# Placing the rows of z in SBUF: blocks of 64, 8, 8, 8 and 2 rows, or five of 16 and one of 10

## The chip, the cores and the metric

The kernel runs on one core of a Trainium2 chip. The metric is the time on the device in microseconds (us). Times come from several runs of the whole kernel and, for the profile, from one execution recorded by the hardware profiler. The core has a matrix engine (PE), three engines for elementwise work (DVE, ACT, POOL), a queue engine (SP) that issues most transfers, and 16 DMA engines that carry them out. SBUF is the on-chip memory of 128 partitions; PSUM takes the results of matmuls.

## The reference

The reference chains two blocks. The first is a long causal convolution by FFT, for each of 8 sequences of 5696 positions and 128 channels; the second is a soft mixture of experts over all 45568 positions with 32 slots and 8 experts. All values are float32.

```python
L = 2 * S
Xf = np.fft.rfft(x, n=L, axis=1); Hf = np.fft.rfft(h, n=L, axis=0)
y = np.fft.irfft(Xf * Hf[None], n=L, axis=1)[:, :S, :]
x = y.reshape(B * S, D)
logits = x @ phi
d = softmax over the positions; slot_input = d.T @ x
slot_out[e] = np.maximum(slot_input[e] @ w1[e], 0) @ w2[e]
c = softmax over the slots;  return c @ slot_out
```

(The two softmax lines are put in words here; each subtracts the maximum and adds 1e-9 to the sum.)

## The kernel before

The transform is done as a two-stage transform with N1 = 90 and N2 = 64, written as matmuls with tables of cosines and sines. Stage A (`load_x`, `fold`, `first_stage`) loads x in chunks of 4 columns, folds them on POOL, multiplies by the table s1 on PE (L217), and stores the result to DRAM as f (L226): 60 rows of 4 KB in each of two stores for the low part, 30 rows in each of four for the high part. Stage B (`load_g`, `stage_b1`, `stage_b2`) loads f back as g (L253), multiplies on PE (L267), multiplies by the spectrum of h on DVE (L285, L294), multiplies on PE again (L309) and stores the result to DRAM as z (L318) in packets of 1 KB. Stage C does the last transform and the experts' softmaxes. It goes by pairs T = 0 to 31, two chunks of one sequence each: four pairs make a sequence.

A pair's z is 90 rows of 16 KB. `load_pair` (L338) loads them into a tile of 128 partitions, "zc", by one DMA for every block that `z_blocks` (L18) lists: first row r, number of rows n, first partition p and step between partitions. The rows of the table i1, with which stage_c1 multiplies, are put on the same partitions by `transform_tables` (L54), from the same list, and the table is zero on the partitions without a row. The tile zc is set to zero once, at the start, so the empty partitions contribute zeros. `stage_c1` (L352) then does 16 matmuls per pair (L365), each over the partitions of zc, and combines their results on ACT, DVE and POOL. `stage_c2` transposes on PE (L393), `stage_c3` makes logits, `stage_c4` to `stage_c6` transpose and keep the softmax's parts, and `dispatch` accumulates the slots' inputs (L480).

The work is interleaved by hand. One step t issues the stages in the order of two strings, `ORDER_E = "xXYf1wb5s"` for odd t and `ORDER_O = "zPxXfb26db3m"` for even t: "z" is `load_pair` of the next pair, "P" the loads of g, "x" and "X", "Y" are stage A, "b" is stage B, "1" is stage_c1. Two steps make one pair. All of these DMAs but a few at the start are issued by SP, in program order, and an issue that waits holds up those after it. As long as stages A and B run, `zring` holds one tile, so z of a pair is loaded into the tile from which the pair before was read.

When stages A and B are over, their tiles are given back, and a second tile for z, "zd", is made (L650). Its empty partitions have to hold zeros as well. The kernel uses only the first 96 partitions of it (`used`, L644): `stage_c1` reads `kr = used` partitions when its tile is zn (L354), and of those 96 the six without a row (`held`, L645) are copied from zc by one DMA (L651). After that, `zring` has two tiles; the remaining pairs are loaded alternately into both (L654, L674, L689, L707). The last phase computes the experts and writes the output.

The block list of the kernel before, with n = 90:

```python
left = [(64 + 8 * j, min(8, n - 64 - 8 * j), j, 4) for j in range((n - 57) // 8)]
return [(0, 64, 32, 1)] + left
```

That is rows 0 to 63 on partitions 32 to 95; rows 64 to 71 on partitions 0, 4, ..., 28; rows 72 to 79 on 1, 5, ..., 29; rows 80 to 87 on 2, 6, ..., 30; rows 88 and 89 on 3 and 7.

Of the kernel before, what the change touches and what calls it, by code (L numbers as in the profile page):

```python
# [16 lines left out]

def z_blocks(n):  # L18

    left = [(64 + 8 * j, min(8, n - 64 - 8 * j), j, 4) for j in range((n - 57) // 8)]  # L20
    return [(0, 64, 32, 1)] + left


def transform_tables(S, N1, N2, CH, X0):
# [29 lines left out]
    for r, n, p, step in z_blocks(N1):  # L54
        i1[p:p + (n - 1) * step + 1:step, :, 0:NP] = part[r:r + n]
# [22 lines left out]
def kernel(  # L78
# [24 lines left out]
    nc = tc.nc  # L103
    P = 128
    B, S, D = x.shape
    NSL = moe_phi.shape[1]
    E, _, F = moe_w1.shape
    SPE = NSL // E
    NFC = F // P
    N1, N2 = 90, 64  # L110
# [8 lines left out]
    HP = P // 2  # L119
# [21 lines left out]
    i1 = const.tile([P, 3, HP], F32, name="i1")  # L141
# [31 lines left out]
    def bank():  # L173
        rings.append(rings.pop(0))
        return rings[-1].tile([P, 512], F32, name="bank", tag="bank")
# [146 lines left out]


    zs, ys, Ls, ds = {}, {}, {}, {}
    zn = used = None
    ybufs = [ypool.tile([P, Q * CH, D + 1], F32, name=f"y{i}") for i in range(2)]
    zring = [ypool.tile([P, 2, 2, CH, 2, D], F32, name="zc")]
    lt = ypool.tile([P, CH, 2, HP], F32, name="lt")
# [9 lines left out]
    def load_pair(T):  # L338
        if T >= NT:
            return  # L340
        b, j = divmod(T, NQ)
        t_ = zring.pop(0)
        zring.append(t_)
        w_ = 2 * 2 * CH * 2 * D
        for r, n, p, step in z_blocks(N1):
            nc.sync.dma_start(
                out=t_[p:p + (n - 1) * step + 1:step, :, :, :, :, :].rearrange("k h o n c d -> k (h o n c d)"),
                in_=zd[b].rearrange("q (a r) c d -> (q a) (r c d)",
                                    a=2)[r:r + n, j * w_:(j + 1) * w_])
        zs[T] = t_  # L350

    def stage_c1(T, between):  # L352
        t_ = zs.pop(T)
        kr = used if t_ is zn else P  # L354
        y_ = ybufs.pop(0)
        ybufs.append(y_)

        def part(v, f):
            k = (2 * v + f) * CH
            return y_[:, k:k + CH, 0:D] if f == 0 else y_[:, k + CH - 1:k - 1:-1, 0:D]  # L360

        def product(o, tab, q):
            p = bank()
            for h_ in range(2):
                nc.tensor.matmul(p[h_ * HP:(h_ + 1) * HP, :], i1[0:kr, tab, :],  # L365
                                 t_[0:kr, h_, o, :, q, :], start=True, stop=True)
            return p[:, :].rearrange("p (n d) -> p n d", d=D)

        def fold_out(even, minus, plus):
            nc.vector.tensor_tensor(out=plus, in0=even, in1=minus, op=AL.add)  # L370
            nc.vector.tensor_tensor(out=minus, in0=even, in1=minus, op=AL.subtract)

        b_, a_ = product(0, 1, 1), product(0, 0, 0)
        nc.scalar.activation(part(0, 0), b_, AF.Copy)
        fold_out(a_, part(0, 0), part(1, 0))
        between()
        b_, a_ = product(1, 1, 0), product(1, 2, 1)
        nc.scalar.activation(om[:, :, :], b_, AF.Copy)

        def after():  # L380
            fold_out(a_, om[:, :, :], op[:, :, :])
            for v, o_, eng in ((1, op, nc.gpsimd), (0, om, nc.vector if tail else nc.gpsimd)):
                for part_, sign in ((part(v, 1), AL.subtract), (part(v, 0), AL.add)):
                    eng.tensor_tensor(out=part_, in0=part(v, 0), in1=o_[:, :, :], op=sign)  # L384

        ys[T] = y_
        return after
# [182 lines left out]
    for t in range(last_front + 1):  # L570
# [12 lines left out]
        def slot_b():  # L583
# [19 lines left out]
            "d": lambda: dispatch(pair(3)) if pair(3) is not None else None,  # L603
            "b": lambda: slot_b(),
            "1": lambda: after.append(stage_c1(T, lambda: stage_c4(U) if U is not None else None))
            if T is not None else stage_c4(U) if U is not None else None,
            "w": lambda: [a_() for a_ in after],
# [30 lines left out]
        if NA < t <= NA + E:  # L638
# [2 lines left out]


    T = V + 1
    used = sum(z_blocks(N1)[0][1:3])  # L644
    held = slice(N1 // 64 * 8 + 3, used - 64, 4)  # L645
    front.close()
    rings.append(mid.enter_context(tc.tile_pool(name="ps2", bufs=4, space=PSUM)))
    last = work.enter_context(tc.tile_pool(name="last", bufs=1))
    tail["last"] = last
    zn = last.tile([P, 2, 2, CH, 2, D], F32, name="zd")  # L650
    nc.sync.dma_start(out=zn[held, :, :, :, :, :].rearrange("k h o n c d -> k (h o n c d)"),  # L651
                      in_=zring[0][held, :, :, :, :, :].rearrange("k h o n c d -> k (h o n c d)"))
    zring.insert(0, zn)
    load_pair(V + 2)  # L654
    nc.sync.dma_start(out=w1s[:, E - 1, :], in_=moe_w1[E - 1])
# [7 lines left out]
    y_ = tail["pool"].tile([P, Q * CH, D + 1], F32, name="y2", tag="y2", bufs=1)  # L663

    after = stage_c1(T, lambda: stage_c4(V))
    after()
    stage_c5(V)
    list(softmax(V))
    nc.gpsimd.memset(y_[:, :, D:D + 1], 1.0)
    for q in range(Q):  # L670
        r = slice(q * NSL, (q + 1) * NSL)
        nc.gpsimd.tensor_copy(out=rep4[r, :, :],
                              in_=ident[r, r].unsqueeze(1).broadcast_to([NSL, Q, NSL]))
    load_pair(T + 2)  # L674
    assert (B - 1) * NQ == T + 1
    for V in range(T, NT):
# [10 lines left out]
        if N < NT:  # L687
            after = stage_c1(N, lambda: stage_c4(V))
            load_pair(N + 2)  # L689
        else:  # L690
            stage_c4(V)
# [16 lines left out]
        else:  # L708
            for b in range(2 * (V - T - 1), min(2 * (V - T), B - 2)):
                nc.sync.dma_start(out=tail["cT"][:, b, :, :].rearrange("p r j -> p (r j)"),  # L710
                                  in_=cd[b].rearrange("p r j -> p (r j)"))
            for i in range(4 * (V - T - 1), min(4 * (V - T), E), 2):
                nc.sync.dma_start(
                    out=w2s[:, i:i + 2, :, :],
                    in_=moe_w2[i:i + 2].rearrange("e (p c) d -> p e c d", p=P))
# [5 lines left out]
    p = bank()  # L721
# [8 lines left out]
    p = bank()  # L730
# [11 lines left out]
    for g in range(EG):  # L742
        for f0 in range(0, F, FH):
            p = bank()
# [9 lines left out]
    for g in range(EG):  # L754
        for k0 in range(0, NFC, 4):
            p = bank()
            for k in range(4):
# [3 lines left out]
                out=hidT[:, g, k0:k0 + 4, :], in_=p[:, :].rearrange("p (k c) -> p k c", k=4))  # L761
    sop = bank()
    for g in range(EG):
        for k in range(NFC):
            for q in range(Q):
                nc.tensor.matmul(sop[q * NSL:(q + 1) * NSL, 0:D],
                                 hidT[:, g, k, q * NSL:(q + 1) * NSL], w2s[:, g * Q + q, k, :],
                                 start=(g == 0 and k == 0), stop=(g == EG - 1 and k == NFC - 1))
# [3 lines left out]
    p = bank()  # L772
    nc.tensor.matmul(p[:, 0:D], tail["rep4"][:, :, :].rearrange("p q s -> p (q s)"), so[:, :],
                     start=True, stop=True)
# [16 lines left out]
    for b in range(B):  # L791
        w1 = 0
        for n in (1, 2, 4, 4) if b == 0 else (4, 4, 3):
# [11 lines left out]
            for q in range(Q):  # L805
# [8 lines left out]
                out=ov[b, t0:t0 + n * RW * N2, :].rearrange("(w p n) d -> p w (n d)", p=P, n=CH),  # L814
                in_=o_[:, 0:n, :, :].rearrange("p w q d -> p w (q d)"))
            if lone:
                nc.sync.dma_start(
                    out=ov[:, NV * RW * N2:, :].rearrange("b (j n) d -> b j (n d)", n=CH),
                    in_=o_[:, n, :, :].rearrange("p q d -> p (q d)"))
# [29 lines left out]
```

## Time and profile before

| | us |
|---|---|
| median of 3 runs | 864.13 |
| lowest and highest run | 862.6, 869.32 |
| profiled execution, its own time | 866.8 |
| its span, first to last instruction | 864.8 |
| PE busy | 777.0 (90%) |
| DVE busy | 618.1 (71%) |
| ACT busy | 437.7 (51%) |
| POOL busy | 392.6 (45%) |

The transfers that matter here, from the page's list of DMA issues (destination and source, number, size of each): z into zc, 30 of 1024 KB, 90 of 128 KB and 30 of 32 KB; z into zd, 2 of 1024 KB, 6 of 128 KB and 2 of 32 KB; zeros from zc to zd, one of 96 KB. In all, 272 MB are moved in 153244 packets.

Busy time of an engine is the union of its instructions' times. The slices are 40 equal parts of the span, 21.6 us each, with the busy share in tenths. A line such as L365 is a line of the kernel. The chain of waits follows the work that ended last back through what released each step. The idle time of an engine that doesn't set the pace costs nothing.

### The profile page before, as it was taken

The numbers are of one execution on the slowest core, as the hardware profiler recorded it, in microseconds if no ns is written. First come the engines' busy times: TensorE is split into PE (matmuls) and PEld (weight loads), VectorE is DVE, ScalarE is ACT, GpSimd is POOL, SyncE is SP. The second block draws the span as 40 slices with busy tenths as digits, with TensorE's granted clock in tenths as the row PEclk, the third lists the DMA queues.
The fourth block names the chain that finished last, engine by engine and source line by source line (L and its number), as shares of the span: only waits on it lengthen the run. The fifth ranks groups of instructions, "written<-read, shape, count | busy, mean of one in ns | idle before, by whom it ended". The sixth has DMA issues, their size and how long they took to land.

```text
span 864.8 us, 20506 instructions
## 1 busy us (share of the span) xinstructions
PE 777.0 (90%) x7796; PEld 376.9 (44%) x7796; DVE 618.1 (71%) x929; ACT 437.7 (51%) x967; POOL 392.6 (45%) x372
## 2 busy tenths in 40 slices
PE   5888888788999999999999999999987888978882
PEld 1122333234444444444444444444444454445882
DVE  3058877666877878887888788777879886963542
ACT  2432344344656565665566566655644445562531
POOL 4453424245556556665566555556434332541000
PEclk9999999999999999999999999999999889997755
DMA  9888999999999999999999999999987887760998
GB/s 297 265 284 300 317 328 339 336 335 342 329 316 343 341 345 324 346 334 338 322 336 348 329 342 334 344 326 345 349 298 269 285 306 261 273 267 7 370 381 328
DMA packets 153244, 272.00 MB, mean 315 GB/s; under 512 B 11878, under 2 KB 110054, under 8 KB 150005
## 3 DMA queue, kind: packets, MB, share of 16 engines
q1 hardware_dynamic: 152571, 270.38, 90.2%
q8 instruction: 62, 1.02, 0.5%
q10 hardware_dynamic: 576, 0.31, 0.1%
q14 instruction: 35, 0.29, 0.1%
HBM read 142.57 MB, written 127.98 MB: 313 GB/s over the span
## 4 chain that ended last, share of the span: by engine, by line
PE 65%; DVE 13%; DMA 8%; issue 4%; POOL 2%; ACT 1%; SPq 1%; DVEq 0%; ACTq 0%; POOLq 0%
PE bank L217 17%; PE bank L365 13%; PE bank L309 8%; PE bt L267 8%; PE bank L393 6%; DMA out_dram<-o 5%; PE bank L480 3%; DVE p L285 3%; DVE bt L285 3%; DVE yf L294 3%; PE bank L402 2%; DMA zc<-z 2%; PE bank L431 2%; POOL x L206 1%; PE bank L454 1%
## 5 line engine op out<-in xcount | busy, mean ns | idle before, releaser
L206 POOL TENSOR_TENSOR x<-xc 128x512 f32<-128x512 f32 x144 | 180.1, 1274 | 229.6 <-PE bank L217 209.2
L217 PE MATMUL bank<-x,s 128*32 128x512 f32 (+1 forms) x1152 | 229.5, 611 | 17.5 <-POOL x L206 15.8
L315 ACT ACTIVATE zst<-bank 128x512 f32<-128x512 f32 (+1 forms) x184 | 98.6, 585 | 182.2 <-PE bank L309 166.7
L220 ACT ACTIVATE fst<-bank 128x512 f32<-128x512 f32 x216 | 127.5, 598 | 110.7 <-PE bank L217 95.9
L285 DVE TENSOR_TENSOR p<-bt,Hi 128x1024 f32<-128x1024 f32 x96 | 111.3, 1159 | 34.1 <-PE bt L267 33.3
L365 PE MATMUL bank<-zc,i 128*64 128x512 f32 x480 | 118.1, 614 | 8.5 <-DMA f<-fst 5.0
L217 PEld LDWEIGHTS bank<-x,s 128*32 128x32 f32 (+1 forms) x1152 | 55.9, 124 | 158.8 <-issue 74.9
L309 PE MATMUL bank<-yf,vt 64*64 64x256 f32 x1440 | 101.6, 389 | 26.0 <-DVE yf L294 25.8
L294 DVE TENSOR_TENSOR yf<-bt,p 128x512 f32<-128x512 f32 x192 | 119.3, 663 | 3.3
L267 PE MATMUL bt<-gt,wt 64*64 64x256 f32 x1620 | 113.5, 388 | 3.7 <-DMA gt<-f 2.8
L285 DVE TENSOR_TENSOR bt<-bt,Hr 128x1024 f32<-128x1024 f32 x96 | 113.0, 1177 | 0.0
L267 PEld LDWEIGHTS bt<-gt,wt 64*64 64x64 f32 x1620 | 54.0, 132 | 78.2 <-issue 35.3
L384 POOL TENSOR_TENSOR y<-y,op 128x512 f32<-128x512 f32 x64 | 77.9, 1217 | 9.8 <-DVE op L370 6.7
L309 PEld LDWEIGHTS bank<-yf,vt 64*64 64x64 f32 x1440 | 56.6, 135 | 57.0 <-issue 28.9
L370 DVE TENSOR_TENSOR y<-bank,y 128x512 f32<-128x512 f32 x32 | 22.1, 692 | 72.5 <-PE bank L365 69.5
L393 PE MATMUL bank<-ident,y 109*128 109x109 f32 x512 | 63.9, 276 | 1.3 <-DVE y L384 1.0
L384 POOL TENSOR_TENSOR y<-y,om 128x512 f32<-128x512 f32 x54 | 64.0, 1184 | 2.1
L365 PEld LDWEIGHTS bank<-zc,i 128*64 128x64 f32 x480 | 30.4, 137 | 71.9 <-issue 47.5
L393 PEld LDWEIGHTS bank<-ident,y 109*128 109x128 f32 x512 | 53.5, 149 | 17.8 <-issue 11.5
L395 ACT ACTIVATE yt<-bank 128x360 f32<-128x360 f32 x128 | 51.3, 492 | 3.2 <-PE bank L393 3.0
L802 PE MATMUL op<-so,cT 32*128 32x128 f32 x704 | 46.2, 380 | 5.5 <-ACT o L811 5.0
L285 DVE TENSOR_TENSOR p<-bt,turn 128x1024 f32<-128x1024 f32 (+1 forms) x12 | 14.2, 1179 | 47.5 <-PE bt L267 46.7
(95 smaller groups left out, 802.0 us busy)
## 6 DMA issues: line engine op xcount, KB each, us to landing
gt<-f SPq DMA_DIRECT2D x99, 512.0 KB
z<-zst SPq DMA_DIRECT2D x88, 512.0 KB
f<-fst SPq DMA_DIRECT2D x144, 240.0 KB
zc<-z SPq DMA_DIRECT2D x30, 1024.0 KB
xc<-in_x_dram SPq DMA_DIRECT2D x64, 320.0 KB
f<-fst SPq DMA_DIRECT2D x144, 120.0 KB
out_dram<-o SPq DMA_DIRECT2D x16, 1024.0 KB
zc<-z SPq DMA_DIRECT2D x90, 128.0 KB
```

What stands on the lines that cost most here:

```text
L206: nc.gpsimd.tensor_tensor(out=y_[:, :, :], in0=t_[:, 0, :, :], in1=t_[:, 1, ::-1, :], op=AL.subtract if comp else AL.add)
L217: nc.tensor.matmul(p[o * width:(o + 1) * width, :], s1[:, comp + G, k], folded[(c, comp)][:, :, :].rearrange("p n d -> p (n d)"), start=Tr ...
L220: nc.scalar.activation(st[:, :, G, :], p[:, :].rearrange("p (n d) -> p n d", d=D), AF.Copy)
L267: nc.tensor.matmul(bt[q * HP:(q + 1) * HP, a, o, :], wt[r, 2 * i + q, :], t_[r, 2 * o + q, :, :].rearrange("p c d -> p (c d)"), start=True ...
L285: nc.vector.tensor_tensor(out=p_, in0=pv, in1=h_, op=AL.mult)
L294: eng.tensor_tensor(out=y_[r, 0:k, c, :], in0=pv[:, :, c, :], in1=pi[r, 0:k, 1 - c, :], op=op_)
L309: nc.tensor.matmul(bz[q][a * HP:(a + 1) * HP, o * 2 * D:(o + 1) * 2 * D], vt[r, i, a, :], y_[r, a * m + o, :, :].rearrange("p c d -> p (c ...
L315: nc.scalar.activation(st[:, 0:m, q, :], bz[q][:, 0:m * 2 * D].rearrange("p (o x) -> p o x", o=m), AF.Copy)
L365: nc.tensor.matmul(p[h_ * HP:(h_ + 1) * HP, :], i1[0:kr, tab, :], t_[0:kr, h_, o, :, q, :], start=True, stop=True)
L384: eng.tensor_tensor(out=part_, in0=part(v, 0), in1=o_[:, :, :], op=sign)
L393: nc.tensor.transpose(p[:, i * TR:(i + 1) * TR], ys[T][0:TR, k * CH + i, 0:D], ident[0:TR, 0:TR])
L395: nc.scalar.activation(yt[:, k * CH:(k + 1) * CH, :, :], of_tokens(p), AF.Copy)
```

## The change

`z_blocks` is rewritten. Rows 0 to 15 go to partitions 0, 8, ..., 120; rows 16 to 31 to 1, 9, ..., 121; and so on for five blocks of 16; the last 10 rows go to 5, 13, ..., 77. A load of z is thus six DMAs, five of 256 KB and one of 160 KB, and not five DMAs. The rows of the table i1 follow, since `transform_tables` reads the same list. All of the 128 partitions are now in the range that has rows, so `used` and `kr` go, and stage_c1 reads 128 partitions of the second tile too. The empty partitions, 38 of them, are 85, 93, ..., 125 (six), 6, 14, ..., 126 (sixteen) and 7, 15, ..., 127 (sixteen); their zeros are copied to the second tile by three DMAs in place of one.

```diff
 def z_blocks(n):
-    left = [(64 + 8 * j, min(8, n - 64 - 8 * j), j, 4) for j in range((n - 57) // 8)]
-    return [(0, 64, 32, 1)] + left
+    return [(r, min(16, n - r), r // 16, 8) for r in range(0, n, 16)]
...
-    zn = used = None
...
     def stage_c1(T, between):
         t_ = zs.pop(T)
-        kr = used if t_ is zn else P
...
-                nc.tensor.matmul(p[h_ * HP:(h_ + 1) * HP, :], i1[0:kr, tab, :],
-                                 t_[0:kr, h_, o, :, q, :], start=True, stop=True)
+                nc.tensor.matmul(p[h_ * HP:(h_ + 1) * HP, :], i1[:, tab, :],
+                                 t_[:, h_, o, :, q, :], start=True, stop=True)
...
     T = V + 1
-    used = sum(z_blocks(N1)[0][1:3])
-    held = slice(N1 // 64 * 8 + 3, used - 64, 4)
+    empty = sorted(set(range(P)) - {p + step * k for _, n, p, step in z_blocks(N1) for k in range(n)})
+    held = [[p for p in empty if p % 8 == c] for c in range(8)]
...
-    nc.sync.dma_start(out=zn[held, :, :, :, :, :].rearrange("k h o n c d -> k (h o n c d)"),
-                      in_=zring[0][held, :, :, :, :, :].rearrange("k h o n c d -> k (h o n c d)"))
+    for ps in held:
+        if ps:
+            r = slice(ps[0], ps[-1] + 1, 8)
+            nc.sync.dma_start(out=zn[r, :, :, :, :, :].rearrange("k h o n c d -> k (h o n c d)"),
+                              in_=zring[0][r, :, :, :, :, :].rearrange("k h o n c d -> k (h o n c d)"))
```

## The prediction

> **What bounds the kernel now.** I read first the page's span and slices, then the busy time by stretch, then the timeline of PE and of SP's queue around one load of z, and last the chain of waits where z is on it. The slices of the page:
>
> ```profile
> span 864.8 us, 20506 instructions
> PE   5888888788999999999999999999987888978882
> PEclk9999999999999999999999999999999889997755
> DMA  9888999999999999999999999999987887760998
> ```
>
> PE and the DMA engines are both at 9 from the sixth slice to the thirtieth: two candidates for the bound over the same stretch. The busy time by stretch (us; busy and count for each engine, then PE clock, DMA share, GB/s) narrows it:
>
> ```profile
> 200.00:620.00 420.00, 416.97 (x4300) 194.66 (x4300) 337.88 (x519) 251.32 (x572) 247.04 (x229) 1.00 0.97 336
> 620.00:720.00 100.00, 85.53 (x894) 46.17 (x896) 83.33 (x130) 48.38 (x112) 34.28 (x35) 0.90 0.85 294
> 720.00:770.00 50.00, 42.84 (x359) 21.32 (x358) 40.71 (x70) 27.20 (x73) 24.84 (x30) 0.96 0.81 305
> ```
>
> PE has 3 us of idle time in 420, at full clock: it sets the pace there. From the first L365 matmul of one pair to that of the next the trace has 20.26 us for pairs 2 to 22, almost without change. But DMA stands at 0.97 beside it, so the cover is thin. How thin the timeline shows (SP's queue, then PE; start, length, line):
>
> ```profile
> 289.32 3.24 SPq L346 DMA_DIRECT2D zc<-z  x5
> 292.60 2.14 SPq L253 DMA_DIRECT2D gt<-f  x3
> ...
> 295.99 3.79 PE L217 MATMUL bank<-x,s 128*64 128x512 f32 x24
> 299.71 0.65 PE L365 MATMUL bank<-zc,i 128*64 128x512 f32 x2
> ```
>
> z of the next pair is issued at 289.32, and its consumer, L365 in stage_c1, starts at 299.71. In the trace's DMA packets (a row of z is one packet of 16,384 bytes, median 0.63 us, 0.61 undisturbed) the last row of a pair ends 8.15 us after the first issue (median, pairs 2 to 22), and L365 starts 1.46 us after that. In pairs 11, 15 and 19 L365 did wait (0.78, 0.31, 0.18 us), though the last packet had ended 0.6 to 1.3 us before; so about 0.6 us passes between packet and release, and the true slack is some **0.85 us**. z has one buffer in that phase, so it can't be issued a pair earlier. Where the pipeline fills, z is already the last to arrive (chain of waits):
>
> ```profile
> 171.14 5.14 DMA zc<-z
> 177.05 3.67 PE bank L365 x16
> ...
> 190.79 6.26 DMA zc<-z
> 197.66 2.42 PE bank L365 x8
> ```
>
> Those two waits cost PE 2.64 and 2.34 us of idle time before L365; at 642.06 there is a third of 2.30.
>
> [...] in a load of z first 16 row packets are in flight, then 8 for about 2 us, then one or two, while 1 KB packets of the next transfer fill the other half; a store of f with 60 rows has 15 in flight. [...] at 40.0 us a store of f from partitions 0 to 59 starts with next to nothing beside it,[...] and of its first 49 packets 34 took 0.24 to 0.31 us, most 0.304, where the median of such packets is 0.159[...]. [...] The trace has half-clock windows of 3.4 us at 110.2, 154.6 and 199.0, none until 642.7, just after the gap at 642.06.
>
> **The change, part by part.**
>
> *Rows by engine.* Before: 64 rows give 4 to each engine, three blocks of 8 one more to engines 0 to 7 each, the last 2 one to engines 0 and 1: 8, 7 or 4 rows. After: six for engines 0 to 9, five for the rest. At 0.63 us this takes 5.1 us down to 3.8 on the fullest engine. That is the gain.
>
> *Rows by port.* [...] a shared row takes 2 x 0.61 = 1.22 us[...]. I take **6.9**, against 5.1 now: z lands 1.8 us later (1.4 to 2.2).
>
> *Steady stretch, pairs 2 to 22.* Bound from below by latency: 1.8 - 0.85 = +0.95 us for a pair. Bound by work per engine: in 220 to 620 us the packets took, per engine and 20.26 us, 9.1 us (1 KB: g and z stores), 1.9 (2 KB: x[...]), 4.3 (4 KB: f, on 15 engines), 15.3 in all; in stretches of 1 KB packets 16 to 19 are in flight on 16 engines, so some 7% of 9.1 is overlap: 14.7. With z at 5.1 and 0.4 for its slow first packet engines 0 and 1 are at 20.2 of 20.26 now. After: 14.7 + 6.9 + 0.4 = 22.0, +1.7 for a pair. With undisturbed packets (14.1 in place of 14.7, as a slower stream disturbs itself less) +1.15. I take **+1.4**; the cases aren't added, since PE's wait and the engines' work are the same time. 21 x 1.4 = +29.4. What follows z in SP's queue (g, x, f, z stores) starts later by as much and is late next.
>
> *Pairs 0, 1 and 23* wait for z already: 3 x 1.8 = +5.4. *Pairs 24 to 27:* distance from last packet to L365 is 1.2, 2.5, 3.0 and 1.5, less 0.6; 1.8 later costs 1.2, 0, 0 and 0.9: +2.1.
>
> *Tail.* The copy of zeros (L651) has 6 rows now, 0.77 us of SP and packets of 0.83 to 0.96. After: 6, 16 and 16 rows in three issues,[...] 2.4 to 3.7 us, some 2.2 later, with two issues of 0.6 inside that. Pair 28's z follows it: 2.2 + 1.8 = 4.0 against 2.65 of slack (729.98 to 733.24, less 0.6): +1.35. Pair 30: 1.8 against 0.8: +1. Pair 29: 5.8 against 5.3: +0.5. Pair 31 has 8 us. Loads of cT and w2 move too, into a slice with 7 GB/s: 0. Sum +2.9.
>
> *Edits costed at nothing.* One more issue of z on SP: 0.54 (64 rows) or 0.61 (8 rows), so 0 to +0.6 for a pair; SP's issues take 257 of 420 us, and the DMA engines run behind it: 0 while they are the later ones. Matmuls of the second buffer over 128 rows, not 96: the tile views have
>
> ```profile
> L365 PE MATMUL bank<-zc,i x480: 592/592/1116, 177.0 to 761.1; 128*64 128x512 f32 x160
> L365 PE MATMUL bank<-zd,i x32: 592/592/1116, 733.2 to 750.6; 96*64 96x512 f32 x32
> ```
>
> with 592 ns each (columns: count, ns least, median, most), so 0. A sixth landing to wait for on PE: no row prices it; under 0.05 us by the 17 ns semaphore steps on SP. Bytes of z are the same.
>
> **Sum:** 29.4 + 5.4 + 2.1 + 2.9 = 39.8 us. The profiled execution took 866.8 us (span 864.8 and 2.0 around it), so 906.6; it is 2.7 above the median of the runs, 864.13, which gives **904**.
>
> **Rivals.** *Writes don't share a port's pace (faster or the same).* For it: x loads with up to 14 engines in flight at 0.084 us. [...] Then only balance is left: z lands 1.2 us or more earlier, pairs 0, 1 and 23 gain 1.2 to 1.8 of their waits (-4.5), pairs 11, 15, 19 their 1.3, PE keeps the rest: -5 (-3 to -8), 859. It decides as soon as a shared row stays under about 0.85 us: six rows then equal the 5.1 of today. *Sharing half hidden:* partners drift apart by more than 0.6 us, or other rings' packets fall between; rows at 0.95, 5.7 + 0.3: +0.3 to +0.9 for a pair, +8 to +24 in all, about 880. *Worse than the sum:* the wait opens gaps in PE, and half-clock windows return; one every 44 us, as before 200 us, loses 1.7 us of PE each, some 17 us over 430 us, on top of +2.1 for a pair: 925 to 940. *The change doesn't spread as said:* if the rows were placed on engines otherwise, the counts in flight would show it; nothing before speaks for it, and its time is that of no port relief, inside the range.
>
> **From cases to numbers.** Chances: the sum 0.50, half hidden 0.17, no port limit 0.20, worse 0.13. About 1% (8.6 us) is what can be told from no change. Faster takes a quarter of the no-limit case, 0.05; the same its rest and a little of the half hidden, 0.20; slower 0.75. Range 858 to 932: it leaves out the lower part of the no-limit case (0.08) and the upper of the worse one (0.07). The likeliest case alone is 890 to 918 (+1.0 to +2.1 for a pair, tail 1 to 5).
>
> **What would show it.** Right: row packets of z near 1.2 us with 16 in flight; last row 9.5 to 10 us after the first issue; pairs 21.5 to 22 us apart; L365 waiting for zc in most pairs; PE's share down by 4 points; copies at 722 us lasting over 2 us. Wrong: rows staying at 0.61 to 0.65 us; the distance still 20.26; or, with long rows, the slack held because z is issued earlier.

## The result and the profile after

The changed kernel takes 937.64 us (median of 4 runs, 936.17 to 938.39) against 864.83 for the kernel before beside it: a ratio of 1.085, 95% interval 1.080 to 1.090. The profiled execution took 936.17, its span is 934.4. The prediction was 904, with a range of 858 to 932. Line numbers are up to three lower in places: L365 is now L362, L346 is L344.

The slices of the page after:

```profile
span 934.4 us, 20542 instructions
PE   5788877779998989998998899989978877788883
PEclk9999998989998999999999999989989889997865
DMA  8899999999999999999999999999998888991799
```

PE has lost its row of nines in the middle; the DMA engines keep theirs, longer than before. The busy time by stretch (columns as before: PE, PEld for PE's weight loads, DVE, ACT, POOL, then PE clock, DMA share, GB/s) says it in numbers:

```profile
200.00:620.00 420.00, 383.74 (x3746) 174.78 (x3747) 295.15 (x456) 221.96 (x502) 217.88 (x203) 0.96 1.02 302
620.00:720.00 100.00, 87.09 (x928) 42.52 (x927) 78.11 (x120) 51.97 (x122) 45.11 (x43) 0.97 0.97 287
720.00:770.00 50.00, 38.91 (x398) 20.70 (x400) 36.65 (x56) 20.04 (x49) 15.27 (x17) 0.86 0.91 274
```

PE is idle for 36 of 420 us where it was idle for 3, and DMA stands at 1.02 (over 1: for 43% of that time the trace has more than 16 packets in flight), while it moves 302 GB/s in place of 336: more engine time, and fewer bytes per us. PE's waits in those 420 us (waiting line, releaser, us, times, longest):

```profile
PE bank L362 <- DMA zc<-z: 29.9, 11, 4.8
PE bank L362 <- DMA f<-fst: 3.3, 1, 3.3
```

Before, the wait of the products for z was 0.5 us in the same window:

```profile
PE bank L365 <- DMA zc<-z: 0.5, 2, 0.3
```

One load of z in SP's queue, and the products that it feeds:

```profile
418.38 4.85 SPq L344 DMA_DIRECT2D zc<-z  x6
...
429.59 3.38 PE L362 MATMUL bank<-zc,i 128*64 128x512 f32 x8 [3.30 <-DMA f<-fst]
```

The six issues take 4.85 us, the products start 11.2 us after the first issue and 3.3 us late, and eight of them take 3.38 us where they take 1.94 at full clock. (The label names f; the packets of this z end at 428.5 and its fifth landing is recorded at 429.06, which is where the chain of waits has it.)

In the trace's packets a row of z takes 1.17 us (median of pairs 2 to 22; 0.63 before) with 16 in flight, the six transfers land some 1.2 us apart, and the last row ends 10.16 us after the first issue (8.33 before). The prediction's 8.15 us for the kernel before, and its 1.46 us from the last row to the products, took in some packets that load instructions and have the same size, 16,384 bytes. Counted by z's rows alone they are 8.33 and 1.25.

From the start of a pair's first product to those of other pairs, the two profiled executions compare so (us):

| stretch | before | after | lost | the prediction's terms |
|---|---|---|---|---|
| start to pair 2 | 219.1 | 227.4 | 8.2 | 3.6 (pairs 0 and 1) |
| pair 2 to 22 | 404.5 | 449.6 | 45.1 | 28.0 (20 x 1.4) |
| pair 22 to 27 | 96.3 | 107.9 | 11.6 | 3.9 (1.8 and 2.1) |
| pair 27 to 31 | 37.5 | 41.3 | 3.8 | 2.9 |
| pair 31 to the end | 107.5 | 108.3 | 0.8 | 0 |

Of the first row 2.2 us were lost ahead of the first load of z. At that point other executions in this study with the same code up to there lie between 2.1 us ahead of the kernel before and 1.9 us behind it, so this is how executions differ. Pairs came 20.22 us apart and now come 22.48 us apart: that is where most of the time went. Two theories went into the experiments. **A**: on the new partitions a row takes 1.17 us in place of 0.63, and with that the 16 engines have more than 22 us of work per pair (22.1 per engine in the trace's packets of 1, 2, 4 and 16 KB from 200 to 620 us), so that they have become the bound. **B**: it is the way of one z, 10.16 us from first issue to last row, that PE waits for, and the stretched products at half clock come on top (37.5 us of half-clock windows between 200 and 620 us, 2.4 before).

### The profile page after: what moved, and what is told of

Read it like the earlier page. It is cut to its first block, busy times and chain, and to the rows that moved or that the text cites. A ratio compares the mean times of both kernels' runs of the same rounds, so it can differ in the third digit from the quotient of the medians.

```text
span 934.4 us, 20542 instructions
## 1 busy us (share of the span) xinstructions
PE 790.6 (85%) x7796; PEld 380.4 (41%) x7796; DVE 619.0 (66%) x929; ACT 437.6 (47%) x967; POOL 392.2 (42%) x372
## 4 chain that ended last, share of the span: by engine, by line
PE 45%; DMA 29%; SPq 8%; DVE 7%; issue 2%; POOL 1%; ACT 1%; DVEq 0%; POOLq 0%
DMA zc<-z 17%; PE bank L362 13%; PE bank L216 10%; SPq L344 7%; PE bt L266 6%; PE bank L308 5%; DMA out_dram<-o 5%; PE bank L390 3%; DMA xc<-in_x_dram 3%; DMA gt<-f 2%; PE bank L428 2%; DMA f<-fst 2%; DVE yf L293 2%; DVE p L284 1%; DVE bt L284 1%
## 5 line engine op out<-in xcount | busy, mean ns | idle before, releaser
L216 PE MATMUL bank<-x,s 128*32 128x512 f32 (+1 forms) x1152 | 224.7, 610 | 16.8 <-POOL x L205 15.6
L362 PE MATMUL bank<-zc,i 128*64 128x512 f32 x480 | 135.6, 691 | 58.5 <-DMA zc<-z 53.3
L367 DVE TENSOR_TENSOR y<-bank,y 128x512 f32<-128x512 f32 x32 | 22.1, 692 | 136.9 <-PE bank L362 131.6
L362 PEld LDWEIGHTS bank<-zc,i 128*64 128x64 f32 x480 | 35.2, 153 | 129.2 <-issue 105.1
L436 POOL MEMSET dt<- 64x8 f32 x32 | 3.4, 106 | 160.2 <-issue 82.2
L390 PE MATMUL bank<-ident,y 109*128 109x109 f32 x512 | 61.6, 269 | 1.0 <-DVE y L381 1.0
L390 PEld LDWEIGHTS bank<-ident,y 109*128 109x128 f32 x512 | 51.4, 145 | 16.3 <-issue 11.2
L371 ACT ACTIVATE y<-bank 128x512 f32<-128x512 f32 x32 | 19.2, 599 | 78.8 <-PE bank L362 78.8
```

Of the source, the lines that this page charges most:

```text
L216: nc.tensor.matmul(p[o * width:(o + 1) * width, :], s1[:, comp + G, k], folded[(c, comp)][:, :, :].rearrange("p n d -> p (n d)"), start=Tr ...
L362: nc.tensor.matmul(p[h_ * HP:(h_ + 1) * HP, :], i1[:, tab, :], t_[:, h_, o, :, q, :], start=True, stop=True)
L390: nc.tensor.transpose(p[:, i * TR:(i + 1) * TR], ys[T][0:TR, k * CH + i, 0:D], ident[0:TR, 0:TR])
```

## Experiments

A ratio is against the kernel before, run beside it; its interval is 95%. "Spacing" is the mean distance of pairs 2 to 22. "Port" in the texts on record is the author's word for something that rows on certain partitions were assumed to share. The traces name neither ports nor partitions, nor the engine that carries a packet: what is measured is the time of a row in each placement, and how many rows are in flight.

### Is it the placement?

**The placement alone.** A kernel of nothing but transfers: four of 16 rows at a time, placed in five ways, first row of 16 KB and then of 2 KB, loads and stores.

```python
LAYOUTS = [("own 4", 32, 4), ("step 8", 0, 8), ("step 4 at 0", 0, 4), ("step 2", 0, 2), ("step 1", 0, 1)]
```

> Computes nothing of the reference: it only moves four transfers of 16 rows at a time between DRAM and SBUF, with nothing beside them, into five layouts: partitions 4 apart from 32[...], 8 apart from 0, 4 apart from 0 and 2 apart from 0[...], 1 apart from 0[...], loads and stores, rows of 16 KB and of 2 KB. Theory of ports: 16 KB rows take 0.61 us, 1.22 to 1.28 us in the three layouts with two on a port, 2.4 to 2.6 us with four, in both directions; 2 KB rows 0.084, 0.16, 0.33. Rival (writes are not limited by the port): 0.61 us for loads in all layouts, more only for stores. Rival (short rows are buffered): loads of 2 KB rows stay at 0.084 us with two on a port.

"Own 4" is the placement for which the forecast has 0.61 us, "step 1" the one with four on a port, and the other three are those with two. Rows of 16 KB (medians): with "own 4" 0.66 to 0.73 us for loads and 0.615 for stores; with steps of 8, of 2, and of 4 from partition 0, 1.25 to 1.28 and 1.27; with step 1, 2.41 and 2.53. So the partitions alone make a row take about twice or four times as long, in either direction, and the forecast's groups hold in these five placements; what lies behind them isn't shown. Rows of 2 KB do not show it: for loads the median is 0.11 to 0.12 us in all five, for stores 0.085 us with "own 4" and 0.085 to 0.11 with the others. Why they don't wasn't tested.

**The layout before, on other partitions.** The block of 64 is put on partitions 0 to 63, the small blocks above it (the copy of zeros follows the layout).

```diff
-    left = [(64 + 8 * j, min(8, n - 64 - 8 * j), j, 4) for j in range((n - 57) // 8)]
-    return [(0, 64, 32, 1)] + left
+    left = [(64 + 8 * j, min(8, n - 64 - 8 * j), 64 + j, 4) for j in range((n - 57) // 8)]
+    return [(0, 64, 0, 1)] + left
```

> The kernel before, with its five transfers and its rows per engine (8, 7 or 4) unchanged; only the partitions differ: the block of 64 rows lies on 0 to 63[...], the blocks of 8 on 64 to 95. Theory[...]: a row of that block takes 1.2 to 1.3 us in place of 0.61, the fullest engine has 4 x 1.25 + 4 x 0.61 = 7.4 us of z as in the changed kernel, L365 waits for zc in most pairs, pairs 21.5 to 22.5 us apart, 910 to 938 us. Rival (the cost is that of more, smaller transfers, of the 64 KB pitch between rows read together, or of the larger copy of zeros): none of these is in this kernel, 862 to 870 us.

985.02 us, ratio 1.141 (1.136 to 1.147): the theory's forecast of 910 to 938 was right in kind, too small in size. Rows take 1.17 us (median), spacing is 24.06, the last row ends 11.97 us after the first issue. The small packets take longer too: those of 1 KB take 0.060 us on the mean, against 0.051 before and 0.055 in the changed kernel. That the eight-row blocks, now on partitions 64 and up, slow the loads of g was the author's guess and isn't shown: the next run moves the block of 64 as well, so it doesn't test it by itself.

**The same with the small blocks left where they were**, the block of 64 on partitions 64 to 127:

```diff
-    return [(0, 64, 32, 1)] + left
+    return [(0, 64, 64, 1)] + left
```

(with zd contracted over 128 partitions, and the empty ones copied in two pieces)

> The kernel before with its block of 64 rows on partitions 64-127[...] but with the rows of 8, 8, 8 and 2 where they were. Five transfers, as before, and no more issues. Theory[...]: rows of the block 1.2-1.3 us, engines 21.2-22.2 us per pair, the fullest of them 7.5 us of z: 900-935, under the first experiment's 985, as the gathered g is not hit. Rival (the cost lies in the 16-row steps or the sixth transfer, not in the port): 860-875, rows at 0.6.

934.19 us, ratio 1.082 (1.077 to 1.087), inside the theory's forecast; spacing 22.40, 1 KB packets 0.052. From 200 to 620 us:

```profile
200.00:620.00 420.00, 384.49 (x3824) 177.12 (x3826) 302.14 (x465) 226.19 (x513) 222.97 (x208) 0.97 0.99 304
```

This is about the whole loss of the changed kernel with five transfers, in the old row order and with no step of 8: **the loss is the placement's**, but for a few us of the longer copy of zeros, which this run has too and which is taken up below. A sixth transfer isn't needed for it.

### Is it the number of issues?

**16-row transfers on the partitions of before**, the small blocks and the copy of zeros as before, eight issues:

```diff
-    return [(0, 64, 32, 1)] + left
+    return [(16 * j, 16, 32 + j, 4) for j in range(4)] + left
```

> The kernel before with its block of 64 rows cut into four transfers of 16 rows, four partitions apart, on the same partitions 32 to 95[...]; the blocks of 8 and 2 stay. Eight issues for a pair, rows read together 64 KB apart. Theory of ports: rows stay at 0.61 to 0.65 us, pairs stay 20.3 us apart, 862 to 870 us. Rival (small transfers, their issue on SP or the pitch cost the time): with eight issues it is at least as slow as the changed kernel with six, 930 us or more.

891.23 us, ratio 1.032 (1.027 to 1.038). Neither forecast: far less than the two placements above cost, more than the theory allowed. Rows take 0.63 us (median), as before; spacing is 21.17. Its SP queue shows what is new:

```profile
405.19 5.70 SPq L346 DMA_DIRECT2D zc<-z  x8
```

Eight issues take 5.70 us where five took 3.24, some 0.7 each, longer than a row (0.63); the last rows can't start earlier, and g is issued later. In 420 us the products wait 11.3 us for z, 6.6 for g and 2.2 for f. So where transfers are quicker than their issues, issues don't seem to be free. That this explains all of the 3% wasn't tested by itself.

**The changed kernel with its sixth transfer issued from ACT:**

```diff
-            nc.sync.dma_start(
+            (nc.sync if n == 16 else nc.scalar).dma_start(
```

> The changed kernel with the sixth transfer (10 rows) issued from ACT, ahead of its work for the next pair. Theory (SP's sixth issue of 0.6 us is hidden behind the 1.25 us that each transfer takes): 928-942, pairs 22.3-22.6 apart. Rival (SP's issue time is on the path, as with eight transfers on own ports): 915-926, pairs 21.8-22.0 apart.

974.32 us, ratio 1.130 (1.124 to 1.136), outside both forecasts. Around 400 us ACT issues the ten rows 7 us after the start of a pair's products, SP the other five 14 us after it, and other waits open (PE, 200 to 620 us):

```profile
PE bank L362 <- DMA zc<-z: 29.7, 11, 4.6
PE bank L362 <- DMA gt<-f: 10.1, 2, 5.7
PE bank L390 <- ACT fst L219: 9.0, 3, 4.5
```

The second and third weren't in the changed kernel. It says what it costs to move this issue to ACT, not what it costs on SP, and leaves that question open. The run with the block on partitions 64 to 127 and five transfers (934) comes within 4 us of the changed kernel, so the sixth transfer seems to cost little; its transfers have other numbers of rows, though.

### What sets the steady pairs: the engines' time, or one z's way?

**z issued earlier.** In the changed kernel, the next pair's z is issued right after the products that free its buffer (not for the first pair of a sequence):

```diff
-    ORDER_E, ORDER_O, XAHEAD = "xXYf1wb5s", "zPxXfb26db3m", 3
+    ORDER_E, ORDER_O, XAHEAD = "xXYf1Zwb5s", "zPxXfb26db3m", 3
...
+            "Z": lambda: load_pair(pair(-2)) if pair(-2) is not None and pair(-2) % NQ else None,
```

> The changed kernel, with z of a pair issued right after stage_c1 of the pair before (some 5 us earlier), except for the first pair of a sequence. Theory A (PE is held up because z lands late; the engines have time for the rest): the waits before L362 go in three pairs of four, 885 to 905 us. Theory B (the engines are out of time: 22 us of packets for each pair): z comes in time but f, g and x come late in its place, pairs stay near 22 us apart, 920 to 938 us.

(In this forecast the letters stand the other way round: its B is A above.) 919.82 us, ratio 1.066 (1.060 to 1.073), at the lower edge of what its B forecast. Spacing is 22.31, hardly less than 22.48. Of the 17.8 us by which the span is shorter, 11.0 lie in pairs 22 to 27 (96.9 us, as in the kernel before), 3.4 in pairs 2 to 22 and 4.3 ahead of them. But in the steady pairs z was not issued earlier: SP reaches the new place only after six f stores, 12.0 us after the start of a pair's products (median), where the changed kernel issues z after 11.2. So for them this run tests neither A nor B.

**Less work for the engines.** Only two of the four column groups of g are loaded, in the changed kernel and in the kernel before; the products on the others read the first two again.

```diff
-        n = sum(k for _, k in us)
+        n = min(2, sum(k for _, k in us))
...
-                                     t_[r, 2 * o + q, :, :].rearrange("p c d -> p (c d)"),
+                                     t_[r, q, :, :].rearrange("p c d -> p (c d)"),
```

> The changed kernel with only the first two of the four column groups of each g unit loaded, the products on the others reading the first two again (half of the transform's input is left out). Takes some 4.3 us of 1 KB packets out of the 22.2 us that the engines are busy per pair. Theory A (engines' time sets the pairs): pairs 20.2-20.8 us apart, time 860-885, not over 25 us above the kernel before with the same left out. Rival B (the way from the first z issue to the last row, 10 us, sets them whatever else runs): still 40 us or more above that. z rows stay at 1.25 us under both.

> The kernel before with the same half of each g unit left out. PE's work is unchanged and bounds it already: 845-862 under both theories; it is what e10 is set against.

875.04 us (ratio 1.010, 1.005 to 1.016) and 848.37 us (0.979, 0.974 to 0.983), 26.7 apart instead of 73. The stretch from 200 to 620 us of the changed kernel with half of g:

```profile
200.00:620.00 420.00, 413.23 (x4268) 191.96 (x4264) 335.68 (x519) 250.44 (x570) 243.07 (x225) 1.00 1.01 297
```

The kernel before, with the same left out:

```profile
200.00:620.00 420.00, 417.88 (x4303) 193.55 (x4301) 338.38 (x521) 253.58 (x577) 244.94 (x228) 1.00 0.87 301
```

In the changed kernel PE is back at 413 of 420 and the spacing at 20.41 (20.15 in the other), though DMA stays at 1.01. And a z still takes its 9.87 us from first issue to last row, with rows of 1.18. **That is the reading that tells A from B:** the way of a z is as long as in the changed kernel, and PE hardly waits for it (5.0 us in 20 pairs). With less for the engines to do, the z issue comes earlier against PE's work, 8.6 us after the start of a pair's products in place of 11.2, and the delay is covered: products start 1.93 us after the last row, 1.18 in the changed kernel. The 1 KB packets fell by 2.4 us per pair and engine, from 9.8 to 7.5 (the forecast took 4.3), and the spacing by 2.1.

One thing these runs don't separate. SP's transfers use eight semaphores in turn (in the kernel before's trace, 840 of 841 issues name the one of the issue eight places before), and an issue waits until that transfer has landed. So SP's queue waits for landings: 179 us of the 420 in the changed kernel, 131 in the kernel before, 134 with half of g. A slow landing of z thus holds up the issues behind it (59 of the 179 us are waits for a z), whether or not the engines are full. That fewer than 15 packets are in flight for only 7% of that stretch in the changed kernel (17% before) speaks for full engines, but no run varied the limit of eight.

Of the 26.7 us that remain, the traces place 5.3 in pairs 2 to 22, 10.3 in pairs 22 to 27, 5.2 in pairs 27 to 31 and 3 at the start: the steady stretch is healed, the rest is another matter.

**Is the half clock a cost of its own?** Products that need no z are put ahead of the first one that does, to keep PE busy where it waited (`idle` is 3 while the front runs):

```diff
+            for _ in range(idle):
+                nc.tensor.matmul(p[0:HP, :], wt[:, 0, :],
+                                 Hr[:, 0:2, :, :, :].rearrange("p w a o d -> p (w a o d)")[:, 0:512],
+                                 start=True, stop=True)
...
-        b_, a_ = product(0, 1, 1), product(0, 0, 0)
+        b_, a_ = product(0, 1, 1, 0 if tail else 3), product(0, 0, 0)
```

> The changed kernel with three more 128x512 products per pair (0.55 us each, 1.65 us in all, while the front runs) ahead of the first product on zc, into a bank that the product then overwrites; they need no z, so they fill part of the wait before it. Theory A (the DMA engines' time sets the pairs, the half-clock windows only follow from waiting): windows at half clock in 200-620 fall from 37 us to under 10, but the time stays at 930-940, with the wait before the products as long as the work leaves over. Rival B (the half clock is a cost of its own, 13 us of stretched products in 20 pairs): the time falls to 915-928.

931.45 us, ratio 1.076 (1.069 to 1.083). No half-clock window is left between 200 and 620 us, but three products were too much to tell anything. The busy time of that stretch:

```profile
200.00:620.00 420.00, 417.65 (x3891) 187.41 (x3893) 298.68 (x460) 223.50 (x505) 220.19 (x205) 1.00 1.01 303
```

PE is full again, with work that was added. So once more with one:

> The changed kernel with one extra 128x512 product per pair ahead of the first product on zc (some 0.8 us of PE's time, as the three of the run before took 2.45 us per pair and by that filled PE, at 22.67 us per pair, so that they told nothing). PE then needs 21.0 us per pair. Theory A (the DMA engines need 22.2 us per pair, half-clock windows only follow from the wait): pairs 22.0-22.6 apart, time 928-938, with or without half-clock windows. Rival B (the stretched products are a cost of their own): as the windows go, pairs 21.4-21.9 apart and 912-926.

931.76 us, ratio 1.081 (1.075 to 1.088). The same stretch:

```profile
200.00:620.00 420.00, 397.45 (x3835) 179.31 (x3836) 300.82 (x464) 224.53 (x508) 220.66 (x207) 0.98 1.02 303
```

PE's wait for z in it (us, times, longest):

```profile
PE bank L366 <- DMA zc<-z: 22.2, 15, 2.4
```

Half-clock windows fall from 37.5 to 13.7 us, PE still waits 22 us, and the spacing stays at 22.54, as A had it. Time that the products win back is waited away. In the steady stretch the half clock is a consequence, not a cost. It follows the waits: in the changed kernel and in this run each half-clock window between 200 and 620 us begins 2.2 to 4.1 us after the start of an idle gap of PE, and these gaps are 2.1 to 4.8 us long. (From pair 22 to 27 these two runs take 101.7 and 102.3 us in place of 107.9: there the half clock seems to be a cost. The next section shows why that part is different.)

### What happened after pair 22?

**The changed layout from pair 22 on.** Pairs 0 to 21 are laid out as before, and i1 is loaded anew once pair 21's products are done (the building of the second table is left out here).

```diff
-        for r, n, p, step in z_blocks(N1):
+        for r, n, p, step in (z_before if T < 22 else z_blocks)(N1):
...
+        if T == 21:
+            nc.scalar.dma_start(out=i1[:, :, :], in_=t_i1)
```

> Rows laid out as in the kernel before up to pair 21 (table i1 is loaded anew after pair 21's products), as in the changed kernel from pair 22 on. The prediction's own terms for that part, 2.1 + 1.8 us for pairs 23 to 27 and 2.9 us for the tail, give 868-873. Theory: the changed kernel really loses some 16 us from pair 22 on (11.6 to pair 27, 4.7 after it), whatever went before: 876-882. Rival: that loss was brought along from the stretch before (clock windows and stores out of step), and the part alone costs under 6 us: 862-868.

887.74 us against 867.71 beside it, ratio 1.022 (1.016 to 1.028): some 20 us, more than either forecast. In its trace pairs 22 to 27 take 110.4 us (96.3 before) and pairs 27 to 31 43.4 (37.5). So these losses are the layout's own there, not brought along. The changed kernel's chain of waits in that part (start, length, what; lines between left out):

```profile
726.73 0.90 SPq L344
...
730.20 8.47 DMA zc<-z
738.67 0.14 issue
738.81 2.81 PE bank L362 x8
...
742.66 2.12 PE bank L362 x8
744.78 1.02 PE bt L266 x16
...
746.70 1.09 ACT zst L314 x2
747.82 0.36 SPq L317
...
748.23 0.50 SPq L636
748.82 0.91 SPq L344
```

It closes on itself: issue of z, landing, products, the z store's source, the store in SP's queue, a load of w1, and the next issue of z, 22.09 us on. Here PE's other work doesn't cover anything: what z takes longer lies on the loop whole, and so do products at half clock (2.81 for eight), as the store comes after them.

**z of pairs 23, 25, 26 and 27 ahead of that store**, the pairs before as in the changed kernel. "Z" stands in the order string where it stood for z issued earlier:

```diff
...
+            "Z": lambda: load_pair(pair(-2)) if pair(-2) is not None and pair(-2) > 22 and pair(-2) % NQ else None,
```

> The changed kernel, with z of pairs 23, 25, 26 and 27 issued right after the products of the pair ahead, instead of behind the z store and the w1 load in SP's queue; the 22 pairs before as they were. Theory (in pairs 23-27 a loop SP store, w1, z issue, 10 us of landing, products, b, zst, store sets the pace, and the late z and its half-clock windows lie on it whole): from pair 22 to 27 96-99 us instead of 107.9, time 924-931. Rival (the engines' time sets these pairs as well): 105 us or more, 934-940.

922.91 us, ratio 1.070 (1.064 to 1.076), 14.7 below the changed kernel and a little better than the theory's forecast. SP's queue around one of these pairs:

```profile
714.72 1.39 SPq L637 DMA_DIRECT2D w1s<-in_moe_w_dram  x1
719.20 3.81 SPq L344 DMA_DIRECT2D zc<-z  x6
723.11 0.40 SPq L317 DMA_DIRECT2D z<-zst  x1
```

z now stands ahead of the store, and pairs 22 to 27 take 91.7 us, 16.2 less than in the changed kernel. The loop was the cause there. The pairs before are unchanged (spacing 22.53), and pairs 27 to 31 take 2.9 us more.

**The longer copy alone.** The kernel before, with zd over 128 partitions and 38 rows of zeros copied in place of 6:

```diff
-    used = sum(z_blocks(N1)[0][1:3])
-    held = slice(N1 // 64 * 8 + 3, used - 64, 4)
+    used = P
+    held = [slice(N1 // 64 * 8 + 3, 32, 4), slice(96, 112), slice(112, P)]
...
```

> The kernel before with zd contracted over all 128 partitions and the copy of 6 rows made 38 (6, 16 and 16 rows in three issues), rows laid out as before. The prediction gave the copies 2.2 to 2.9 us of its sum. Theory (the tail's loss comes from the slower z of pairs 28 and 29, as in the run with the changed layout from pair 22 on, and the copies have slack): 0 to +2 us, within 0.3%. Rival (the copies push pair 28's z behind them): +2.5 to +5 us.

871.99 us, ratio 1.010 (1.006 to 1.015): about +7 us, the rival's +2.5 to +5 or more. SP's queue in the kernel before:

```profile
722.35 0.77 SPq L651 DMA_DIRECT2D zd<-zc  x1
723.17 3.17 SPq L346 DMA_DIRECT2D zd<-z  x5
```

And with the longer copy:

```profile
726.75 2.02 SPq L652 DMA_DIRECT2D zd<-zc  x3
728.82 6.53 SPq L346 DMA_DIRECT2D zd<-z  x5
```

Copies and the five issues of pair 28's z take 8.6 us in place of 4.0, the rows of that z 104 us in sum in place of 72, and pairs 27 to 31 42.0 in place of 37.5: 4.5 us, about what the tail of the changed kernel lost (3.8). In the four profiles with the short copy and z's block on partitions 32 to 95 this stretch took 35.6 to 37.5. The rest of the 7 us, 4.6 of it in pairs 2 to 22, lies in pairs whose code is as before; single executions differ by as much.

### Versions meant to be faster

**80 rows on partitions 24 to 103 in one transfer, 6 and 4 rows beside them, z early:** 7, 6 or 5 rows to an engine by the author's count.

```diff
-    return [(0, 64, 32, 1)] + left
+    return [(0, n - 10, 24, 1), (n - 10, 6, 104, 4), (n - 4, 4, 0, 4)]
...
```

> A version meant to beat both: 80 rows in one transfer on partitions 24-103, 6 and 4 rows on partitions four apart beside them (7, 6 or 5 rows per engine, three issues), and the next pair's z issued after the products of the pair. Theory: PE stays the bound at 20.2 us per pair, and only the waits of pairs 0, 1 and 23 (7.3 us, with 5 us of stretched products) can go: 852-862. Rival:[...] rows over 0.9 us: 870-890.

885.78 us, ratio 1.027 (1.019 to 1.034): the rival's, with rows of 0.99 us on the mean and a spacing of 21.00. Why these rows take 0.99 isn't shown. Some 7 us more lie in pairs 27 to 31 (44.6 us), where this version copies 38 rows of zeros too.

**The kernel before with early z:**

> The kernel before with z of the next pair issued after the products of the pair, layout unchanged: a version meant to beat both. Theory: PE's 20.2 us per pair stay, and waits of pairs 0, 1 and 23 with their stretched products (some 10 us in the profile of before) go in part: 855-862, 0.2 to 1% less. Rival: z's rows then meet the f stores and the gathered g, which come late in their place: 864-875.

865.02 us, ratio 1.001 (0.9985 to 1.0035): nothing. Here too z was issued no earlier in the steady pairs, 11.5 us after the start of a pair's products where the kernel before issues it after 10.9, so an earlier z is still untested there. No version was found that beats the kernel before.

## Why the prediction was right or wrong

*The rows.* Right: rows near 1.2 us with 16 in flight, L362 waiting for z in most pairs, PE's share down from 90% to 85%. z landed 1.83 us later (10.16 in place of 8.33), and 1.8 was forecast. That a row would take twice as long was an estimate, from the f store at 40.0 us (most packets at 0.304 us against a median of 0.159); six such rows make 7.3 us, less what the author took off for rows out of step. Which rows would slow each other was assumed, and the times bear it out for the placements that were run, no further. The rows for each engine fit the counts in flight: in a load of the kernel before, issued at 350.02, 16 rows at first, 8 or 9 for some 1.5 us, then one; in one of the changed kernel, issued at 372.27, 15 or 16, then 10, then two. Which engine carries which row isn't shown. The first rival, loads without this slowing, is refuted by the bare transfers: loads took 1.25 to 1.28 us and stores 1.27 in the same three placements.

*The steady stretch: the term that failed.* The prediction took +1.4 us for a pair, 29.4 of its sum of 39.8. The pairs lost 2.26. It had two bounds that don't add, latency (+0.95 for a pair) and engines' work (22.0 us, +1.7), with a lower variant of the second (+1.15), and it took a value between them. The experiment with half of g speaks for the second bound, so about a third of the miss, 0.3 us for a pair, is that it took less than it had worked out. The rest, 0.5 us, it did not have. It put the rest of the engines' work at 14.7 us, to shrink if anything, "as a slower stream disturbs itself less". In the changed kernel that work grew: 1 KB packets take 0.055 us on the mean in place of 0.051, which is 9.8 us in place of 9.1 per pair and engine. 22.0 and 0.7 make 22.7, and 22.48 was measured. This is read from the same run afterwards, though, and it isn't steady: in the run with z issued earlier 1 KB packets took 0.050 us, and pairs still came 22.31 us apart. So where the last 0.5 us for a pair come from stays open. Rows of z were not undersized (six of 1.12 us, the mean, are 6.7; 6.9 was taken). The latency bound was: with 1.25 us from the last row to the products, less the 0.5 to 0.8 that passed in pairs 11, 15 and 19, the slack is some 0.6 us, not 0.85, and the bound +1.2.

*Pairs 24 to 27: wrong in kind.* The prediction took each pair's distance between last row and product as slack to be used up once, +2.1 with 1.8 for pair 23. In a loop a pair's delay moves the next issue, so the distance isn't there again, and products at half clock count in full. The loss was 11.6 us in the changed kernel and 14.1 with the layout in that part alone. Pair 23 was misread as well: in the kernel before its wait was ended by DVE, 0.4 us after z had landed.

```profile
642.06 3.09 PE L365 MATMUL bank<-zc,i 128*64 128x512 f32 x8 [2.30 <-DVE df L421]
```

*Tail.* +2.9 stated, 3.8 lost, and the copies can account for it, as stated: 4.5 us by themselves. But the run with the block on partitions 0 to 63, whose copy is short, lost 9.0 us there, so a slow z costs in the tail too, and how the two share the 3.8 isn't shown.

*Pairs 0 and 1.* 3.6 stated; 6.0 lost once 2.2 us ahead of any z are taken off. Of pair 1's 16 products ten took over 1.0 us, four before.

*At nothing.* The wider matmuls: 592 ns in both tile views, right. The sixth issue: not isolated.

*The rivals.* The time lies where "worse than the sum" had it, 925 to 940, but that is luck, as its mechanism isn't what was found. It gave 17 us to half-clock windows. They came, for 37.5 us, and no cost of theirs was found in the steady stretch; only from pair 22 to 27 did they seem to count, with some 6 us. The missing time was that of the steady pairs' +2.26 and of the loop. Half-hidden sharing is refuted: rows were not at 0.95 but at 1.17.

The stretches lost 69.5 us against 38.4 of terms beside them (the sum has 1.4 more, for one further pair): 17 short in the steady stretch, 8 in pairs 22 to 27, 6 in the rest, of which 2.2 belong to no edit.

## What to carry to other kernels

In this kernel, balance of rows over DMA engines was worth less than a good placement over partitions: by the count of rows, six of 1.17 us on the fullest engine lose to eight of 0.63. Where the DMA share is at 0.97 beside a full PE, add up the engines' work per round before and after. Here that sum (+1.7 us) came nearer to the measured +2.26 than the slack in one transfer's way did (+0.95), and a value between the two was worse than the sum; it was still 0.5 us short. And follow the chain of waits round once: if it returns to the same queue entry, a delay in it is paid in every round. In pairs 22 to 27, moving the late load ahead of what follows from its own products won more (16.2 us) than the longer load had cost (11.6).

## What the runs showed of the hardware

- The time of a 16 KB row went by the partitions of the 16 rows of a transfer, with nothing beside it: on 32, 36, ..., 92 a row took 0.66 to 0.73 us in loads and 0.615 in stores; on 0, 8, ..., 120, on 0, 4, ..., 60 and on 0, 2, ..., 30 it took 1.25 to 1.28 and 1.27; on 0 to 15 it took 2.41 and 2.53. Rows of 2 KB took 0.11 to 0.12 us in loads on all five.
- In the whole kernel a row of z took 0.63 us (median) with the block of 64 on partitions 32 to 95, and 1.17 with it on 0 to 63 and in the changed kernel.
- 1 KB packets, which carry no row of z, took 0.051 us on the mean before, 0.055 in the changed kernel, 0.052 with the block of 64 on partitions 64 to 127, 0.060 with it on 0 to 63, and 0.050 in the changed kernel with z issued earlier. What sets this isn't shown.
- Half-clock windows of 37.5, 20.5 and 13.7 us in 420 (the changed kernel, the one with z ahead of the store from pair 23 on, the one with one product more) went with the same spacing, 22.48 to 22.54 us: in this stretch, where PE waits for DMA, PE's clock did not set the time.
- Half-clock windows between 200 and 620 us began 2.2 to 4.1 us after the start of an idle gap of PE of 2.1 to 4.8 us, in the changed kernel and in the one with one product more.
- Moving one ten-row transfer per pair from SP's queue to ACT's raised the time by 37 us.
